# Attention output of odd head pairs in the other partition half, in a fused attention and two-layer MoE kernel on one core

## Chip, core and metric

One core of one Trainium2 chip runs the whole program in one launch. The metric is the device time of an execution in microseconds; lower is better. Before the change the median of 3 runs is 480.46 us (479.46 to 480.7).

## What is computed

Three stages follow each other, all with float32 inputs and results (w_in and w_out come as float64).

```python
# 1. decayed linear attention, B=2, H=8, S=768, D=64, in blocks along S
intra = (q_b k_b^T * Dmask) v_b                 # Dmask[i,j] = lam^(i-j), j<=i
inter = (q_b * lam^(pos+1)) kv_state
out_b = intra + inter
kv_state = lam^block * kv_state + (k_b * lam^(block-1-pos))^T v_b
# 2. x = out as [1536, 512]; x = act(x @ w_in) @ w_out
#    act(h) = h if h>=1, 0 if h<=-1, (h+1)^2/4 between;  w_in [512, 2048], w_out [2048, 512]
# 3. each token goes to the best of 8 experts: gate * relu(x @ w1[e]) @ w2[e]
```

## The kernel before

**Stages and chunks.** The 1536 tokens are 12 attention blocks of 128 tokens (six for each batch; all 8 heads of a block are one tile row). Blocks 0 to 3, 4 to 7 and 8 to 11 are three chunks of 512 tokens. For each chunk the first MoE (units 0 to 23, eight for a chunk, two tiles of 128 hidden columns each) runs a first layer (`m1_l1`, L700 to L709) and a second layer (`m1_l2`, L738 to L745), one unit behind. Each product is made of three matmuls, high by high, high by low and low by high part, in a fast float32 format; so every operand exists as a high and a low tile (xh and xl for the attention's output, w1h and w1l for w_in). Then tokens are routed, and the experts' tiles follow (`Tile2`).

**Weights of the first MoE.** w_in and w_out come as float64 in groups of 1 MB, [128 partitions, 8 KB]. `load_w` (L205) loads a group, and `convert` makes float32 of it: ScalarE L223 and L225, VectorE L226 (first pass, into cu) and L232 (second pass, into cw). `hilo` splits it: ScalarE L212 writes w1h, VectorE L213 writes w1l. The converted group is stored to DRAM (L239, issued by ScalarE) and read again for chunks 1 and 2. The first group of w_in is converted after block 2's xh and xl (`issue_after`), and its second pass stays behind the masks of block 4 (`behind[1, 0]`, L873).

**One attention block** (`attn_pieces`) has these steps. Heads come in four pairs, `pr`; head `h2` of a pair has its 64 channels in partition half `h2` of q and k.

- `prep`: GpSimd makes the decayed keys kd (L279) and the decayed queries qd (L288; three instructions, L290 and twice L293, for blocks from SWAP = 7 on).
- `masked`: eight matmuls of scores (L308) into two PSUM tiles, and two masks am on VectorE (L311). Three am buffers exist.
- `outv`: the value products, am by v (L335), into the output's PSUM tile.
- `outs`: the state products, state of the block before by qd (L348), added into the same tile; then xh on ScalarE (L354) and xl on VectorE (L355).
- `st`: the key-value products (L377) into a PSUM tile of their own, and the new state on VectorE, four instructions (L383), or a copy on ScalarE for the first block of a batch (L380). The last block of a batch (5, 11) makes no state.

A state product uses 64 rows and 64 columns of TensorE's array. Up to block 6 both heads of a pair keep their half, so only two of the four quarters of the array are used. From block 7 on the state and qd of the odd pairs lie in the other half, so the four pairs take turns over four quarters, with two PSUM tiles. For that, block 6's key-value products of odd pairs go to the other half, qd is written there in pieces, and `lamx` holds the decay in the changed order (three VectorE copies, L364 to L366).

**Order.** TensorE's order is the program's own (`manual_schedule`). The other engines' order comes from a planner that takes, as an engine falls free in its own reckoning, the earliest instruction of the program that is ready. The opening (L860 to L876) runs blocks 0 to 4: scores are issued one block ahead, then for a block m: key-value products, value products, scores of block m+1, state products. In block 0 the key-value products come after the output. Here PSUM tiles come from six buffers in turn (`at_tags`). After the opening, blocks 5 to 11 are cut in up to four pieces (`return [scores, st, outp, None]`), which `spread` places among the matmuls of the first and second layers; PSUM tiles then come from two buffers. Each piece is a visit: TensorE leaves the full tiles of the layers for the smaller ones of the attention and returns.

The queue of loads starts as `q1 v0 v1 q2 v2 q3 v3 w10 q4 v4 w11 w20` after q0, all on SP's queue; w10 is w_in's group 0 and v4 the keys and values of block 4.

Of the kernel before, what the change touches and what calls it, by code (L numbers as in the profile page):

```python
# [37 lines left out]
NSTART = 5  # L38
WARM_LAM = 6

SWAP = 7
START_LOADS = "q1 v0 v1 q2 v2 q3 v3 w10 q4 v4 w11 w20"

WHOLE = (2, 0)
# [3 lines left out]
def kernel(  # L48
# [129 lines left out]
    lamx = small([P, 4, 1], "lamx")  # L178

# [15 lines left out]
    def load_w(k, n):  # L195
        if n >= len(units):
            return
        lay, c, g = units[n]
        if lay == 2:
            load_raw((k, n), (w1 if k == 1 else w2)[bass.ds(tiles[c].e, 1), g])  # L200
        elif c:
            load_raw((k, n), wsc[k, g])
        else:
            t = sb.tile([P, 1024, 2], I32, name=f"rw{k}", tag=f"rw{k}")
            SP.dma_start(out=t.rearrange("p n t -> p (n t)"), in_=(w_in if k == 1 else w_out)[g].bitcast(I32))  # L205
            raw[k, n] = t

    def hilo(key, r, eng):
# [60 lines left out]
    def attn_pieces(m):  # L269
# [3 lines left out]
        def prep():  # L273
            if m >= NSTART - 1 and m + 1 < NBLK:
                load_attn(m + 1)
            qkt, kvt = attn_in[m]
            def keys():
                kd = sb.tile([P, NE, 64], F32, name="kd", tag="kd")
                G.tensor_tensor(kd, kvt[:, 0], rev.to_broadcast([P, NE, 64]), op=ALU.mult)  # L279
                ast[m, "kd"] = kd  # L280


            if cb < 5 and m >= NSTART:
                keys()
            if cb > 0:
                qd = sb.tile([P, 4, P], F32, name="qd", tag="qd")
                if m < SWAP:
                    G.tensor_tensor(qd, qkt[:, 0], wq, op=ALU.mult)  # L288
                else:
                    G.tensor_tensor(qd[:, 0::2, :], qkt[:, 0, 0::2, :], wq[:, 0::2, :], op=ALU.mult)  # L290
                    for h2 in range(2):
                        r, o = slice(64 * h2, 64 * h2 + 64), slice(64 - 64 * h2, 128 - 64 * h2)
                        G.tensor_tensor(qd[o, 1::2, :], qkt[r, 0, 1::2, :], wq[r, 1::2, :], op=ALU.mult)  # L293
                ast[m, "qd"] = qd
            if cb < 5 and m < NSTART:
                keys()
# [5 lines left out]
        def masked():  # L302
# [6 lines left out]
            for h2 in range(2):  # L309
                am = sb3.tile([P, 4, P], F32, name="am", tag="am")  # L310
                ast[m, "am"] = V.tensor_tensor(am, pts[h2], dmask.rearrange("p (r o) i -> p r o i", o=2)[:, :, h2, :], op=ALU.mult)  # L311
                ast[m, "A", h2] = am

        def outv():
# [8 lines left out]
            if m < SWAP:  # L323
                pt = at_tile([P, 4, P], "ao")
                pts, first, last = [pt[:, pr, :] for pr in range(4)], (0,), (3,)
                ast[m, "o"] = pts, [(pt, slice(0, 4))]
            else:
                two = [at_tile([P, 2, P], "ao") for _ in range(2)]
                pts, first, last = [two[pr % 2][:, pr // 2, :] for pr in range(4)], (0, 1), (2, 3)
                ast[m, "o"] = pts, [(two[i], slice(i, 4, 2)) for i in range(2)]  # L330
            ast[m, "last"] = last
            for pr in range(4):
                for h2 in range(2):
                    r = slice(64 * h2, 64 * h2 + 64)
                    PE.matmul(  # L335
                        pts[pr][r], lhsT=kvt[:, 1, 2 * pr + h2, :], rhs=am[h2][:, pr, :],
                        start=(pr in first), stop=(cb == 0 and pr in last), skip_group_check=True,
                    )

        def outs():  # L340
            pts, banks = ast.pop((m, "o"))
            last = ast.pop((m, "last"))
            if cb > 0:
                for pr in range(4):
                    for h2 in range(2):
                        r = slice(64 * h2, 64 * h2 + 64)
                        w = r if m < SWAP or pr % 2 == 0 else slice(64 - 64 * h2, 128 - 64 * h2)
                        PE.matmul(  # L348
                            pts[pr][r], lhsT=state[m - 1][w, pr, :], rhs=ast[m, "qd"][w, pr, :],
                            start=False, stop=(pr in last), skip_group_check=True,  # L350
                        )
            sl = slice(j * P, (j + 1) * P)
            for pt, prs in banks:
# [3 lines left out]
        def outp():  # L357
            outv()
            outs()

        def st():
            if m == NSTART:
                with tc.issue_after(ast[m, "am"].ins):
                    V.tensor_copy(lamx[:, 0::2], lamc[:, 0::2])  # L364
                    V.tensor_copy(lamx[64:128, 1::2], lamc[0:64, 1::2])
                    V.tensor_copy(lamx[0:64, 1::2], lamc[64:128, 1::2])  # L366
            if cb == 5:
                return
            qkt, kvt = attn_in[m]
            kd = ast.pop((m, "kd"))  # L370
            pt = at_tile([P, 4, 64], "as")
            for pr in range(4):
                for h2 in range(2):
                    h = 2 * pr + h2
                    at_ = 64 * h2 if m < SWAP - 1 or pr % 2 == 0 else 64 - 64 * h2
                    r = slice(at_, at_ + 64)
                    PE.matmul(pt[r, pr, :], lhsT=kd[:, h, :], rhs=kvt[:, 1, h, :], start=True, stop=True)  # L377
# [10 lines left out]
        pieces[m] = (prep, masked, outv, outs)  # L388
# [471 lines left out]
    for m in range(2):  # L860
        pieces[m][0]()
    for m in range(NSTART):
        if m:
            pcs[m][3]()
        pieces[m][2]()
        if 0 < m < NSTART - 1:
            pcs[m + 1][0]()
        pieces[m][3]()
        if not m:
            pcs[m][3]()  # L870
        if m == 3:

            behind[1, 0] = ast[4, "am"]  # L873
# [257 lines left out]
```

## Time and profile before

| what | us |
|---|---|
| median of 3 runs | 480.46 |
| lowest, highest | 479.46, 480.7 |
| profiled execution | 479.74 |
| its span | 477.9 |
| TensorE matmuls busy in it | 464.0 |
| VectorE, ScalarE, GpSimd busy | 328.0, 266.7, 81.3 |

PE is TensorE's matmuls, PEld its weight loads, DVE VectorE, ACT ScalarE, POOL GpSimd, SP the engine that issues most DMAs. In a line of the timeline stand the start in us from the span's start, the time from the first start to the last end of the group, the engine, the line of the program, the operation, what it writes and reads, its shape, how many instructions are merged, and in brackets the idle time before it and what ended that. Each matmul of the program counts as two.

### The profile page before, as it was taken

What the parts mean: (1) busy time and instruction counts of PE and PEld (TensorE: products, weight loads), DVE (VectorE), ACT (ScalarE), POOL (GpSimd) and SP (SyncE); (2) the same over time, 40 slices, a digit from 0 to 9 for tenths busy, and PEclk for the clock granted to TensorE, in tenths of its full rate; (3) what the DMA queues carried; (4) which work ended last, traced back from release to release, by engine and by line L of the source; (5) the groups of instructions that cost most, each with busy time, mean ns of one, the idle gap of its engine ahead of it and who ended that gap; (6) DMA issues with size and microseconds to landing.
All of it is one profiled execution on the core that took longest, in us unless ns stands there. A gap on an engine that the chain in (4) does not pass through costs nothing. (4 is left out here: it accounts for less than half of the span.)

```text
span 477.9 us, 7360 instructions
## 1 busy us (share of the span) xinstructions
PE 464.0 (97%) x2713; PEld 377.7 (79%) x2713; DVE 328.0 (69%) x726; ACT 266.7 (56%) x403; POOL 81.3 (17%) x83
## 2 busy tenths in 40 slices
PE   8999999999999999999999999999999999999990
PEld 5875778878878787878888888887878998998870
DVE  6889979879399997464999785666874354444410
ACT  2388879868975455445756754667233435435320
POOL 4513210002003120000000007000164400400201
PEclk9999999999999999999999999999999999999996
DMA  8999987768564223221433235330456543543201
GB/s 336 423 408 375 394 310 254 291 243 253 195 218 171 95 89 133 87 84 64 163 123 98 89 100 188 104 138 1 175 179 197 177 162 103 188 141 111 87 1 48
DMA packets 22651, 83.65 MB, mean 175 GB/s; under 512 B 3595, under 2 KB 3595, under 8 KB 20564
## 3 DMA queue, kind: packets, MB, share of 16 engines
q1 hardware_dynamic: 15842, 65.04, 38.9%
q10 hardware_dynamic: 4322, 11.55, 6.2%
q0 software_dynamic: 2448, 6.56, 3.9%
q8 instruction: 22, 0.36, 0.3%
q14 instruction: 17, 0.14, 0.1%
HBM read 68.44 MB, written 14.73 MB: 174 GB/s over the span
## 5 line engine op out<-in xcount | busy, mean ns | idle before, releaser
L213 DVE TENSOR_TENSOR w2l<-rw,w2h 128x1024 fp32r<-128x1024 f32 x32 | 39.2, 1225 | 55.2 <-ACT w2h L212 55.1
L700 PE MATMUL l<-xh,w1h 128*128 128x512 f32 x192 | 75.3, 397 | 0.9 <-ACT w1h L212 0.6
L743 PE MATMUL acc<-w2h,gh 128*128 128x512 f32 x184 | 72.8, 396 | 0.0
L702 PE MATMUL l<-xl,w1h 128*128 128x512 f32 x184 | 71.7, 390 | 0.0
L703 PE MATMUL l<-xh,w1l 128*128 128x512 f32 x184 | 71.7, 390 | 0.0
L745 PE MATMUL acc<-w2h,gl 128*128 128x512 f32 x184 | 71.7, 390 | 0.0
L744 PE MATMUL acc<-w2l,gh 128*128 128x512 f32 x184 | 71.7, 389 | 0.0
L212 ACT ACTIVATE w2h<-rw 128x1024 fp32r<-128x1024 f32 x32 | 33.9, 1059 | 57.1 <-PE m2a L819 30.0
L449 DVE CUSTOM_DVE_ANT_0 jk<-x2s,enb 128x512 f32<-128x512 f32 x72 | 48.0, 699 | 0.8 <-ACT x2s L434 0.6
L726 ACT ACTIVATE gh<-g_t 128x512 fp32r<-128x512 f32 x46 | 28.9, 629 | 33.0 <-DVE g_t L722 33.0
L213 DVE TENSOR_TENSOR w1l<-rw,w1h 128x1024 fp32r<-128x1024 f32 x32 | 39.7, 1241 | 11.1 <-ACT w1h L212 10.2
L719 ACT ACTIVATE r_t<-l,half 128x512 f32<-128x512 f32 x48 | 32.4, 680 | 26.2 <-PE l L703 25.8
L794 PE MATMUL m<-x2h,w1h 128*128 128x384 f32 (+2 forms) x128 | 43.9, 343 | 0.0
L700 PEld LDWEIGHTS l<-xh,w1h 128*128 128x128 f32 x192 | 35.8, 188 | 10.1 <-ACT w1h L212 1.2
L796 PE MATMUL m<-x2h,w1l 128*128 128x384 f32 (+2 forms) x128 | 43.3, 338 | 0.0
L795 PE MATMUL m<-x2l,w1h 128*128 128x384 f32 (+2 forms) x128 | 43.1, 337 | 0.0
L722 DVE SCALAR_TENSOR_TENSOR g_t<-r_t,l 128x512 f32<-128x512 f32 x46 | 31.4, 682 | 16.1 <-ACT r_t L720 16.0
L817 PE MATMUL m2a<-w2h,mh 128*128 128x512 f32 (+1 forms) x104 | 41.5, 399 | 0.0
L819 PE MATMUL m2a<-w2h,ml 128*128 128x512 f32 (+1 forms) x104 | 40.8, 392 | 0.0
L743 PEld LDWEIGHTS acc<-w2h,gh 128*128 128x128 f32 x184 | 34.5, 188 | 7.8 <-issue 0.5
L818 PE MATMUL m2a<-w2l,mh 128*128 128x512 f32 (+1 forms) x104 | 40.7, 391 | 0.0
L703 PEld LDWEIGHTS l<-xh,w1l 128*128 128x128 f32 x184 | 34.6, 188 | 7.2
(252 smaller groups left out, 843.9 us busy)
## 6 DMA issues: line engine op xcount, KB each, us to landing
rw<-wsc SPq DMA_DIRECT2D x32, 512.0 KB, 3.4
rw<-in_w_dram SPq DMA_DIRECT2D x32, 512.0 KB, 3.9
rw<-in_w_in_dram SPq DMA_DIRECT2D x8, 1024.0 KB
rw<-in_w_out_dram SPq DMA_DIRECT2D x8, 1024.0 KB, 12.8
wsc<-cw ACTq DMA_DIRECT2D x15, 512.0 KB, 6.8
qk_t<-in_qk_dram SPq DMA_DIRECT2D x12, 512.0 KB, 5.3
kv_t<-in_kv_dram SPq DMA_DIRECT2D x12, 512.0 KB, 12.5
x2d<-x2s ACTq DMA_DIRECT2D x12, 256.0 KB, 2.9
```

What stands on the lines that cost most here:

```text
L213: wlo[key] = eng.tensor_tensor(lo, r, hi.bitcast(F32), op=ALU.subtract)
L449: V.tensor_tensor_reduce(out=jk, in0=x2s, in1=enb[e // 2][:, e % 2, :], scale=1.0, scalar=0.0, op0=ALU.mult, op1=ALU.add, accum_out=lr[:, ...
L700: PE.matmul(pt, lhsT=hi[:, f, k, :], rhs=xh[c][:, k, :], start=(k == 0), stop=False)
L702: PE.matmul(pt, lhsT=hi[:, f, k, :], rhs=xl[c][:, k, :], start=False, stop=False)
L703: PE.matmul(pt, lhsT=lo[:, f, k, :], rhs=xh[c][:, k, :], start=False, stop=(k == 3))
L743: PE.matmul(a, lhsT=gh[:, f, sl], rhs=hi[:, f, :], start=(g == 0 and f == 0), stop=False)
L744: PE.matmul(a, lhsT=gh[:, f, sl], rhs=lo[:, f, :], start=False, stop=False)
L745: PE.matmul(a, lhsT=gl[:, f, sl], rhs=hi[:, f, :], start=False, stop=(g == 7 and f == 1))
L794: PE.matmul(pt, lhsT=hi[:, f, k, :], rhs=self.xh[:, k, :], start=(k == 0), stop=False)
L795: PE.matmul(pt, lhsT=hi[:, f, k, :], rhs=self.xl[:, k, :], start=False, stop=False)
L796: PE.matmul(pt, lhsT=lo[:, f, k, :], rhs=self.xh[:, k, :], start=False, stop=(k == 3))
L817: PE.matmul(a, lhsT=gh[:, f, sl], rhs=hi[:, f, :], start=(g == 0 and f == 0), stop=False)
```

## The change

All blocks get the order of quarters that only late blocks had, by another way: the state stays where it is, and the output of the odd pairs is written to the other partition half (`turned`). So xh and xl hold the odd pairs' channels with their halves exchanged, and the rows of w_in that they meet are exchanged as well, by its load: one transfer for the even row groups, two for the odd ones. Every block now has two output banks. The key-value products go into the unused half of the second bank, at the start of the output's visit, and the new state is made after xh and xl in that visit. In the opening block 0 has the order of the other blocks. `lamx`, SWAP and the split of qd are gone.

```diff
 load_w:
-            SP.dma_start(out=t.rearrange("p n t -> p (n t)"), in_=(w_in if k == 1 else w_out)[g].bitcast(I32))
+            if k == 1:
+                src = w_in[g].bitcast(I32).rearrange("p (f k x) -> p f k x", f=2, k=4)
+                dst = t.rearrange("p (f k i) t -> p f k (i t)", f=2, k=4)
+                SP.dma_start(out=dst[:, :, 0::2, :], in_=src[:, :, 0::2, :])
+                for h2 in range(2):
+                    r, o = slice(64 * h2, 64 * h2 + 64), slice(64 - 64 * h2, 128 - 64 * h2)
+                    SP.dma_start(out=dst[o, :, 1::2, :], in_=src[r, :, 1::2, :])
+            else:
+                SP.dma_start(out=t.rearrange("p n t -> p (n t)"), in_=w_out[g].bitcast(I32))
 prep:
-                if m < SWAP:
-                    G.tensor_tensor(qd, qkt[:, 0], wq, op=ALU.mult)
-                else:
...
+                G.tensor_tensor(qd, qkt[:, 0], wq, op=ALU.mult)
 attn_pieces:
+        def st():
+            banks = [at_tile([P, 4, P], "ao") for _ in range(2)]
+            ast[m, "banks"] = banks
+            if cb == 5:
+                return
...
+            pt = banks[1][:, 2:4, :].rearrange("p a (b d) -> p (a b) d", d=64)
...
+                    PE.matmul(pt[r, pr, :], lhsT=kd[:, h, :], rhs=kvt[:, 1, h, :], start=True, stop=True, skip_group_check=True)
+        def turned(pr, h2):
+            o = 64 * (h2 ^ (pr % 2))
+            return slice(o, o + 64)
 outv, outs:
+                for h2 in ((0, 1), (1, 0))[pr % 2]:
-                        pts[pr][r], lhsT=kvt[:, 1, 2 * pr + h2, :], rhs=am[h2][:, pr, :],
+                        banks[pr % 2][turned(pr, h2), pr // 2, :], lhsT=kvt[:, 1, 2 * pr + h2, :], rhs=am[h2][:, pr, :],
-                            pts[pr][r], lhsT=state[m - 1][w, pr, :], rhs=ast[m, "qd"][w, pr, :],
+                            banks[pr % 2][turned(pr, h2), pr // 2, :], lhsT=state[m - 1][r, pr, :], rhs=ast[m, "qd"][r, pr, :],
 after xh and xl, in outs:
+            pt = ast.pop((m, "st"))
             sn = sb.tile([P, 4, 64], F32, name="s_new", tag="state")
...
-                        sn[:, pr, :], state[m - 1][:, pr, :], (lamc if m < SWAP else lamx)[:, pr, :], pt[:, pr, :], op0=ALU.mult, op1=ALU.add,
+                        sn[:, pr, :], state[m - 1][:, pr, :], lamc[:, pr, :], pt[:, pr, :], op0=ALU.mult, op1=ALU.add,
-        return [scores, st, outp, None] if m >= NSTART else [scores, None, outp, st]
+        return [scores, None, outp, None]
 opening:
-        if m:
-            pcs[m][3]()
-        pieces[m][2]()
+        pieces[m][2]()
+        pieces[m][3]()
         if 0 < m < NSTART - 1:
             pcs[m + 1][0]()
-        pieces[m][3]()
-        if not m:
-            pcs[m][3]()
+        pieces[m][4]()
```

## Rows read from the trace of the kernel before

**Rows 1.** Page, part 1: busy time, share of the span, instructions.

```profile
PE 464.0 (97%) x2713; PEld 377.7 (79%) x2713; DVE 328.0 (69%) x726; ACT 266.7 (56%) x403; POOL 81.3 (17%) x83
```

**Rows 2.** Waits of TensorE: waiting line, what for, us in total, times, longest.

```profile
PE l L700 <- ACT w1h L212: 0.6, 1, 0.6
PE l L700 <- DVE g_t L722: 0.2, 1, 0.2
```

**Rows 3.** Timeline of TensorE, 10.7 to 25.2 us.

```profile
...
15.38 1.40 PE L308 MATMUL sc<-qk_t 64*128 64x128 f32 x16
16.70 1.09 PE L348 MATMUL ao<-qd,s_new 64*64 64x128 f32 x16
17.72 0.69 PE L377 MATMUL as<-kv_t,kd 128*64 128x64 f32 x16
18.24 1.05 PE L335 MATMUL ao<-am,kv_t 128*64 128x128 f32 x16
19.21 1.40 PE L308 MATMUL sc<-qk_t 64*128 64x128 f32 x16
...
22.72 1.09 PE L335 MATMUL ao<-am,kv_t 128*64 128x128 f32 x14 [0.17 <-DVE am L311]
...
24.94 0.50 PE L700 MATMUL l<-xh,w1h 128*128 128x512 f32 x1
```

**Rows 4.** Timeline of VectorE, 11 to 25 us.

```profile
11.29 0.85 DVE L383 SCALAR_TENSOR_TENSOR s_new<-s_new,lamc,as 128x64 f32<-128x64 f32 x4
...
16.62 1.29 DVE L311 TENSOR_TENSOR am<-sc,dmask 128x512 f32<-128x512 f32 x2 [0.55 <-PE sc L308]
18.46 0.28 DVE L383 SCALAR_TENSOR_TENSOR s_new<-s_new,lamc,as 128x64 f32<-128x64 f32 x1 [0.55 <-PE as L377]
18.66 0.68 DVE L355 TENSOR_TENSOR xl<-ao,xh 128x512 fp32r<-128x512 f32 x1
...
21.39 1.28 DVE L311 TENSOR_TENSOR am<-sc,dmask 128x512 f32<-128x512 f32 x2
22.59 1.21 DVE L232 SCALAR_TENSOR_TENSOR cw<-cz,cu 128x1024 int32<-128x1024 int32 x1
23.72 0.68 DVE L355 TENSOR_TENSOR xl<-ao,xh 128x512 fp32r<-128x512 f32 x1
```

**Rows 5.** Timeline of ScalarE, 18 to 31 us.

```profile
18.34 1.24 ACT L223 ACTIVATE cu<-rw,down 128x1024 int32<-128x1024 uint32 x1
...
23.83 1.06 ACT L212 ACTIVATE w1h<-cw 128x1024 fp32r<-128x1024 f32 x1 [1.55 <-DVE cw L232]
...
30.71 0.69 ACT L719 ACTIVATE r_t<-l,half 128x512 f32<-128x512 f32 x1 [1.36 <-PE l L703]
```

**Rows 6.** Timeline of TensorE, the output of block 7.

```profile
106.03 0.67 PE L348 MATMUL ao<-qd,s_new 64*64 64x128 f32 x16
106.62 0.50 PE L743 MATMUL acc<-w2h,gh 128*128 128x512 f32 x1
```

**Rows 7.** Timeline of TensorE, the visit of block 8's key-value products.

```profile
133.92 0.39 PE L700 MATMUL l<-xh,w1h 128*128 128x512 f32 x1
...
135.05 0.39 PE L703 MATMUL l<-xh,w1l 128*128 128x512 f32 x1
135.37 0.69 PE L377 MATMUL as<-kv_t,kd 128*64 128x64 f32 x16
...
136.78 0.39 PE L700 MATMUL l<-xh,w1h 128*128 128x512 f32 x1
```

**Rows 8.** Instructions on the tile lamx: ns min/median/max, first and last start.

```profile
L366 DVE COPY lamx<-lamc x1: 165/165/165, 36.4 to 36.4; 64x2 f32<-64x2 f32 x1
```

**Rows 9.** DMA queue of SP, 6 to 11.5 us, 4 KB packets: packets, MB, share.

```profile
q1 hardware_dynamic: 623, 2.26, 101.6%
```

**Rows 10.** The same, 18.9 to 21.9 us, 8 KB packets.

```profile
q1 hardware_dynamic: 173, 1.29, 102.4%
```

**Rows 11.** Timeline of GpSimd: the decayed keys of block 4.

```profile
19.34 1.04 POOL L279 TENSOR_TENSOR kd<-kv_t,rev 128x512 f32<-128x512 f32 x1 [3.20 <-DMA kv_t<-in_kv_dram]
```

More of the change, by code (lines that the diff above doesn't have):

```diff
@@ L39 @@
 WARM_LAM = 6
-SWAP = 7
 START_LOADS = "q1 v0 v1 q2 v2 q3 v3 w10 q4 v4 w11 w20"
@@ L177 @@
     lamc = small([P, 4, 1], "lamc")
-    lamx = small([P, 4, 1], "lamx")
     units = [(1, c, g) for c in range(len(CHUNKS)) for g in range(8)]
@@ L286, in prep @@
                 qd = sb.tile([P, 4, P], F32, name="qd", tag="qd")
-                if m < SWAP:
-                    G.tensor_tensor(qd, qkt[:, 0], wq, op=ALU.mult)
-                else:
[L290 to L293, printed above, removed]
+                G.tensor_tensor(qd, qkt[:, 0], wq, op=ALU.mult)
                 ast[m, "qd"] = qd
@@ L312, in masked @@
                 ast[m, "A", h2] = am
+        def st():
[3 more added lines that the diff above has]
+                return
+            kvt = attn_in[m][1]
+            kd = ast.pop((m, "kd"))
+            pt = banks[1][:, 2:4, :].rearrange("p a (b d) -> p (a b) d", d=64)
+            ast[m, "st"] = pt
+            for pr in range(4):
+                for h2 in range(2):
+                    h = 2 * pr + h2
+                    r = slice(64 * h2, 64 * h2 + 64)
+                    PE.matmul(pt[r, pr, :], lhsT=kd[:, h, :], rhs=kvt[:, 1, h, :], start=True, stop=True, skip_group_check=True)
+        def turned(pr, h2):
+            o = 64 * (h2 ^ (pr % 2))
+            return slice(o, o + 64)
         def outv():
@@ L320, in outv @@
             am = [ast.pop((m, "A", i)) for i in range(2)]
[L323 to L330, printed above, removed]
@@ L331, in outv @@
-            ast[m, "last"] = last
+            banks = ast[m, "banks"]
             for pr in range(4):
-                for h2 in range(2):
-                    r = slice(64 * h2, 64 * h2 + 64)
+                for h2 in ((0, 1), (1, 0))[pr % 2]:
                     PE.matmul(
-                        pts[pr][r], lhsT=kvt[:, 1, 2 * pr + h2, :], rhs=am[h2][:, pr, :],
-                        start=(pr in first), stop=(cb == 0 and pr in last), skip_group_check=True,
+                        banks[pr % 2][turned(pr, h2), pr // 2, :], lhsT=kvt[:, 1, 2 * pr + h2, :], rhs=am[h2][:, pr, :],
+                        start=(pr < 2), stop=(cb == 0 and pr >= 2), skip_group_check=True,
@@ L338, in outv @@
                     )
         def outs():
-            pts, banks = ast.pop((m, "o"))
-            last = ast.pop((m, "last"))
+            banks = ast.pop((m, "banks"))
             if cb > 0:
                 for pr in range(4):
-                    for h2 in range(2):
+                    for h2 in ((0, 1), (1, 0))[pr % 2]:
                         r = slice(64 * h2, 64 * h2 + 64)
-                        w = r if m < SWAP or pr % 2 == 0 else slice(64 - 64 * h2, 128 - 64 * h2)
                         PE.matmul(
-                            pts[pr][r], lhsT=state[m - 1][w, pr, :], rhs=ast[m, "qd"][w, pr, :],
-                            start=False, stop=(pr in last), skip_group_check=True,
+                            banks[pr % 2][turned(pr, h2), pr // 2, :], lhsT=state[m - 1][r, pr, :], rhs=ast[m, "qd"][r, pr, :],
+                            start=False, stop=(pr >= 2), skip_group_check=True,
@@ L351, in outs @@
                         )
             sl = slice(j * P, (j + 1) * P)
-            for pt, prs in banks:
+            for i in range(2):
+                pt, prs = banks[i][:, 0:2, :], slice(i, 4, 2)
                 ast[m, "xh"] = A.activation(xh[c][:, prs, sl], pt, AF.Copy)
                 ast[m, "xl"] = V.tensor_tensor(xl[c][:, prs, sl], pt, xh[c].bitcast(F32)[:, prs, sl], op=ALU.subtract)
[L357 to L366, printed above, removed]
@@ L367, in st @@
             if cb == 5:
                 return
[L369 to L377, printed above, removed]
+            pt = ast.pop((m, "st"))
@@ L383, in st, with outp @@
                     V.scalar_tensor_tensor(
-                        sn[:, pr, :], state[m - 1][:, pr, :], (lamc if m < SWAP else lamx)[:, pr, :], pt[:, pr, :], op0=ALU.mult, op1=ALU.add,
+                        sn[:, pr, :], state[m - 1][:, pr, :], lamc[:, pr, :], pt[:, pr, :], op0=ALU.mult, op1=ALU.add,
                     )
             state[m] = sn
-        pieces[m] = (prep, masked, outv, outs)
-        return [scores, st, outp, None] if m >= NSTART else [scores, None, outp, st]
+        def outp():
+            st()
+            outv()
+            outs()
+        pieces[m] = (prep, masked, st, outv, outs)
+        return [scores, None, outp, None]
     def inv_norm(s, n, nm, over_=None):
```

## The prediction

> **What bounds the kernel now.** I read the page's busy times first: TensorE is busy 97% of the span [rows 1]. A busy TensorE can still stand behind somebody, so the second view was its waits: two matter, 0.6 us for the high half of a w_in tile and 0.2 us for g_t, both before 51 us [rows 2]. After that nothing makes it wait, so from there on every microsecond taken out of its order shortens the run by as much; before, a microsecond counts only if whoever comes next is not late. The third view is therefore the order of TensorE, VectorE and ScalarE up to 25 us [rows 3 to 5], where blocks 0 to 4 of the attention run with nothing else beside them and end in the first matmul of the first layer (L700, 24.94).
>
> In rows 3 one block goes through scores (L308), the state products of the block before (L348), the key-value products for the new state (L377) and the value products (L335). State products occupy TensorE from 16.70 to 17.72, 1.02 us; key-value products 0.52 us (17.72 to 18.24); value products 0.97 us. The period of a block is 3.83 us (15.38 to 19.21). What the reader is to see in rows 4 and 5: L700 starts 0.05 us after ScalarE ends w1h (23.83 plus 1.06), and w1h starts as soon as VectorE is through with its second conversion pass (22.59 plus 1.21). So the end of the opening is set twice, by TensorE's order and by the conversion of the first w_in tile, almost to the same moment.
>
> **State products in four quarters.** Late blocks have them already: 106.03 to 106.62, 0.59 us with the change back to full tiles [rows 6], against 1.02 us in halves [rows 3]. The new placement uses the same four quarters and two banks, so 0.43 us is saved in each of blocks 1 to 5. Block 5 lies inside the first layer (its state products come at about 46 us): 0.43 us kept. In blocks 1 to 4 the 1.72 us are not kept. The next scores' masks are made on VectorE from the scores: from the scores' start to the end of both masks takes 2.53 us (15.38 to 17.91) [rows 3, 4], and the value products need both; with 0.97 us for them a block cannot repeat faster than about 3.55 us. That is 0.28 us less than now, for two periods; in block 0 the value products move behind the key-value products, which delays the mask that waits for their buffer by about 0.35 us. Scores of block 4 start at 19.2 us either way. Its masks are later still, at 21.39, because VectorE's first conversion pass stands ahead of them (their scores are done at 20.61), and TensorE waits for them at 22.72 [rows 3, 4]. So the opening gains nothing up to 22.7 us.
>
> **The new state in the output's visit.** For blocks 6 to 10 the key-value products lose a visit of their own. A visit: 1.73 us from the matmul at 135.05 to the fourth after it, where four steps take 0.90 us (five steps 1.13 us, 133.92 to 135.05), so 0.83 us [rows 7]. Within the output's visit they cost 0.52 us [rows 3]; saved are 0.31 us, five times, 1.55 us. Bounds: 0.7 us if they cost their whole duration of 0.69 us there, 1.9 us if they pack closer.
>
> The state update (L383, four instructions, 0.85 us together [rows 4]) now comes after the state products instead of before them, since it reads a bank that these write. In late blocks the next use is a visit later and TensorE waits for nobody: cost nothing, covered by that distance; without it 0.85 us per block. In the opening it is different. State 3 used to be begun at 18.46 and done by about 20.0, xl in between; now it is ready to be made only after the state products of block 3, at about 21.2, when VectorE is in conversion and masks until 22.67. TensorE wants it at about 23.7 for block 4. Behind the masks stand three things: state 3 (0.85 us), xl of block 3 (0.68 us) and the second conversion pass, which is what w1h and then L700 wait for. The order on VectorE is the planner's. In rows 4 it put one state update (18.46) ahead of xl (18.66), because that waits for ScalarE, and it put conversion (22.59) ahead of xl (23.72). By these rows I take: state 3, conversion, xl. Then conversion, w1h and L700 are 0.85 us later: L700 at 25.8. Ends: 0.25 us if conversion goes first and TensorE waits for state 3 a little; 1.6 us if xl goes ahead too; at best nothing. Once lost it is lost: the next w1h stands on ScalarE behind an activation that itself waits 1.36 us for TensorE (30.71) [rows 5], so all moves together and the wait of 0.6 us in rows 2 stays.
>
> **What else goes.** Three copies to lamx, 0.17 us each [rows 8], leave VectorE at about 35 to 37 us, where it is busy without a break; with them the 0.2 us for g_t [rows 2] go. Splitting qd into three for blocks 7 and up disappears on GpSimd, for which TensorE waits nowhere: nothing, covered by the distance between a block's scores and its output. xh and xl of blocks 0 to 6 come in two halves: one more instruction each on ScalarE and VectorE, under 0.2 us, hidden behind the mask loop in the opening and behind nobody's wait later. The bank with the new state is held until the update; the next scores want it several units later.
>
> **w_in in three transfers.** Rows of 8 KB become pieces of 1 KB, 1024 instead of 128, and SP issues three transfers where it issued one, eight times. No row has 1 KB pieces. With 4 KB packets the 16 engines move 2.26 MB in 5.5 us at 101.6%, so 404 GB/s or 162 ns for a packet on one engine [rows 9]; with 8 KB packets 1.29 MB in 3 us at 102.4%, so 420 GB/s or 312 ns [rows 10]. A line through both has 12 ns a packet and 37.5 ns a KB: 50 ns for 1 KB, 396 instead of 312 ns for a row, and at eight rows to an engine 0.67 us more for each load. Ends: nothing, or double, 2.5 us (a load is 2.5 us now). I take 0.67 us, the line. The first load is read at 18.34 [rows 5]. The value load two places behind it lands at 19.34 [rows 11], and the 1.05 MB between take 2.5 us, so the first load lands at about 16.8, with 1.5 us of cover: hidden. That value load moves to 20.0, its decayed keys on GpSimd to 21.1, where the key-value products of block 4 want them at about the same time while the masks last until 22.67: hidden too. Behind SP's two more issues stands the load of q for block 4, wanted at 19.2, and later loads; their queue is filled well ahead. If a cover goes, the price is what a load is late by.
> The Trainium skill, "DMA: Bandwidth & Descriptors", section Bandwidth, advises at least 1 MiB to a transfer for three quarters of the peak, and gives about 2 us fixed for each; by that two more transfers a load would add 4 us to each of eight loads. The trace does not agree where transfers queue: in rows 9 loads of 512 KB follow each other with the engines full.
>
> **Sum**, against the profiled execution of 479.74 us (span 477.9 and 1.8 around it, 0.72 us under the median of 480.46): block 5 -0.43, five visits -1.55, g_t -0.2, opening +0.85: -1.33. Applied to the median: 479.1 us. A measurement of this kernel can tell about 0.3%, 1.44 us, from no change; so the forecast lies just inside no change.
>
> **Rivals.** (A) The forecast, 0.45, with -0.7 to -2.0 us: 478.5 to 479.8; two fifths of it is beyond 1.44 us.
> (B) The opening gives back little: conversion keeps its place ahead of state 3, and TensorE's wait for that costs 0.25 us or less. Sum -1.9, and -2.5 where the wait of 0.6 us shrinks as well: 478.3. For it: rows 4 show conversion ahead of xl. Against: state 3 is ready over 1 us before VectorE gets to choose. 0.27.
> (C) Slower: the small pieces. Place: the first load, then each next one. It decides from 1.5 us more a load, where the read at 18.34 starts to slip. At double cost the first load is 1.0 us late, and since the engines are full through the opening the lag adds up by 2.5 us a load over the first five, against covers of a few us: some 5 us of waits on ScalarE's conversions, less 2 us of gains, +3 us: 483.5. For it: the full engines in rows 9 and 10, and no row with such pieces. Against: the fixed part of 12 ns. 0.13. By the skill's 2 us a transfer the same mechanism would decide from the first load on; I give that 0.03 of the 0.13.
> (D) VectorE takes both state 3 and xl ahead of conversion, 1.6 us or a little more: -0.6 to 0, 480.1. 0.15.
>
> **How the numbers follow.** Faster: B and two fifths of A, 0.45. Same: the rest of A and D, 0.42. Slower: C, 0.13. The range from 477.8 to 481.6 takes in A, B, D and the milder part of C.
>
> **What would show it.** Right: 16 state products in about 0.6 us in blocks 1 to 5; no L377-like group alone between first- or second-layer matmuls after 60 us; L700 first at about 25.8; block 4's value products waiting for masks as now; packets of the SP queue up by about 7200 and no wait for rw. Wrong: L700 before 24.9 (the opening kept its gain) or after 26.6; ScalarE or VectorE waiting for a w_in load; a new wait of TensorE after 60 us; GpSimd's decayed keys holding block 4.

## The result, and the profile after

The change makes the kernel slower: 487.02 us median (484.43 to 487.96, 4 runs) against 479.96 (479.33 to 480.7, 4 runs) of the kernel before on the same chip, a ratio of 1.0135, interval 1.0108 to 1.0161. I had forecast 479.1 us, and even the upper end of my range, 481.6, is 5.4 us short. The profiled execution took 487.96 us, its span is 486.1 us, so it is read beside a span of 477.9.

The page of the changed kernel comes first: busy time of TensorE, its granted clock in 40 slices of 12.15 us, and GB/s of the DMA engines in the same slices.

```profile
PE 462.7 (95%) x2713; PEld 377.2 (78%) x2713; DVE 328.3 (68%) x730; ACT 267.5 (55%) x410; POOL 73.7 (15%) x73
...
PEclk9999799999999999999999999999999999999996
...
GB/s 315 287 317 335 304 328 309 301 333 291 264 159 177 137 131 52 123 88 83 133 88 131 101 109 182 88 159 14 102 227 177 170 172 130 173 134 119 94 1 46
```

TensorE's matmuls are busy 1.3 us less than in [rows 1], in a span that is 8.2 us longer: the time went into waits. The transfers run at about 300 GB/s for the first ten slices, with the engines no less busy than before, and the clock has a 7 in the fifth slice. The waits of TensorE (line, what it waited for, us in total, times, longest) answer to [rows 2].

```profile
PE l L694 <- DVE g_t L716: 6.2, 2, 5.6
PE ao L328 <- POOL kd L286: 2.5, 2, 1.5
```

The wait for g_t that was 0.2 us is 6.2 us. Where and why is in three timelines. TensorE's own (L328 makes the key-value products, L355 the state products, L694 to L697 the first layer) in two stretches, the end of the opening and 49 to 62 us:

```profile
24.75 0.69 PE L328 MATMUL ao<-kv_t,kd 128*64 128x64 f32 x16 [1.49 <-POOL kd L286]
...
27.04 1.01 PE L355 MATMUL ao<-qd,s_new 64*64 64x128 f32 x16 [0.72 <-DVE s_new L372]
27.98 1.19 PE L694 MATMUL l<-xh,w1h 128*128 128x512 f32 x4
...
49.23 0.39 PE L696 MATMUL l<-xl,w1h 128*128 128x512 f32 x1
...
51.53 0.39 PE L697 MATMUL l<-xh,w1l 128*128 128x512 f32 x1
57.47 0.79 PE L694 MATMUL l<-xh,w1h 128*128 128x512 f32 x1 [5.55 <-DVE g_t L716]
58.06 0.63 PE L696 MATMUL l<-xl,w1h 128*128 128x512 f32 x1
...
61.47 0.63 PE L694 MATMUL l<-xh,w1h 128*128 128x512 f32 x1
```

VectorE's (L233 is the first conversion pass, L239 the second, L363 xl, L372 the new state):

```profile
24.92 1.21 DVE L239 SCALAR_TENSOR_TENSOR cw<-cz,cu 128x1024 int32<-128x1024 int32 x1
26.05 0.74 DVE L363 TENSOR_TENSOR xl<-ao,xh 128x256 fp32r<-128x256 f32 x2
26.72 0.84 DVE L372 SCALAR_TENSOR_TENSOR s_new<-s_new,lamc,ao 128x64 f32<-128x64 f32 x4
...
54.46 1.23 DVE L233 SCALAR_TENSOR_TENSOR cu<-rw,cu 128x1024 int32<-128x1024 int32 x1 [4.23 <-ACT cu L230]
...
56.73 0.68 DVE L716 SCALAR_TENSOR_TENSOR g_t<-r_t,l 128x512 f32<-128x512 f32 x1
```

and the one line of ScalarE's that began it:

```profile
53.21 1.21 ACT L230 ACTIVATE cu<-rw,down 128x1024 int32<-128x1024 uint32 x1 [4.97 <-DMA rw<-in_w_in_dram]
```

It is the longest of three; the list of ScalarE's waits, 0 to 130 us, has for this step (us in total, times, longest):

```profile
ACT cu L230 <- DMA rw<-in_w_in_dram: 8.1, 3, 5.0
```

Read from the bottom of the timelines: ScalarE stood 4.97 us before a load of w_in that had not landed; VectorE's conversion behind it waited 4.23 us for ScalarE; g_t stood behind the conversion on VectorE's queue, and TensorE waited 5.55 us for g_t. The opening lost time as well: block 4's key-value products waited 1.49 us for their keys (24.75), which GpSimd began at 23.24 where it had begun them at 19.34 [rows 11], because their load came later. The next row of TensorE's timeline shows a second price. Eight matmul steps take 3.41 us from 58.06 to 61.47, 0.43 us each; ten steps took 2.30 us from 49.23 to 51.53, 0.23 us each. The windows of the changed kernel say why (columns: us, then busy time of PE, PEld, DVE, ACT and POOL with their instructions, PEclk, DMA share, GB/s).

```profile
12.00:25.00 13.00, 10.20 (x182) 8.45 (x184) 9.49 (x22) 4.62 (x9) 8.48 (x7) 1.00 1.10 286
25.00:38.00 13.00, 12.28 (x102) 9.96 (x99) 12.37 (x22) 9.71 (x12) 1.28 (x1) 1.00 1.07 314
...
57.40:62.00 4.60, 4.53 (x11) 3.56 (x12) 4.60 (x7) 4.54 (x6) 0.00 (x0) 0.50 1.03 322
62.00:70.00 8.00, 8.00 (x37) 6.62 (x36) 5.28 (x7) 5.35 (x8) 0.00 (x0) 1.00 1.08 305
```

From 57.4 to 62 us the granted clock was 0.50, the level of 1.2 GHz, behind a wait of 5.55 us; after that 2.4 GHz again. Ten steps at 0.2 us more are 2.0 us. The first two lines are where the cause lies; the first of these windows in the kernel before was:

```profile
12.00:25.00 13.00, 12.72 (x209) 10.84 (x207) 10.57 (x23) 5.14 (x7) 6.83 (x6) 1.00 1.03 424
```

Full engines in both, 424 GB/s in the one and 286 in the other. The DMA view of 12 to 38 us shows the loss in 40 slices of 0.65 us; changed kernel:

```profile
GB/s 403 389 367 362 183 158 233 228 238 228 266 359 383 375 355 307 200 192 241 247 222 228 331 378 391 403 391 397 425 410 391 372 356 172 169 227 238 301 211 260
```

It isn't slow throughout: mostly 350 to 425 GB/s, with three dips to 160 to 250, and three loads of w_in come up in the queue there. In the six slices from 14.6 us on the mean is 211 GB/s, 0.82 MB in 3.9 us; at the 403 GB/s of other slices that takes 2.0 us. So I estimate 1.9 us lost in that dip; the next (six slices from 22.4 us, mean 222) lost 1.8 us by the same working.

### The profile page after: what moved, and what is told of

Read it like the earlier page. It is cut to its first block, busy times and chain, and to the rows that moved or that the text cites. A ratio compares the mean times of both kernels' runs of the same rounds, so it can differ in the third digit from the quotient of the medians.

```text
span 486.1 us, 7386 instructions
## 1 busy us (share of the span) xinstructions
PE 462.7 (95%) x2713; PEld 377.2 (78%) x2713; DVE 328.3 (68%) x730; ACT 267.5 (55%) x410; POOL 73.7 (15%) x73
## 5 line engine op out<-in xcount | busy, mean ns | idle before, releaser
L694 PE MATMUL l<-xh,w1h 128*128 128x512 f32 x192 | 76.1, 401 | 6.2 <-DVE g_t L716 6.2
L697 PE MATMUL l<-xh,w1l 128*128 128x512 f32 x184 | 72.4, 393 | 0.0
L694 PEld LDWEIGHTS l<-xh,w1h 128*128 128x128 f32 x192 | 36.4, 190 | 15.6 <-DVE g_t L716 7.0
L697 PEld LDWEIGHTS l<-xh,w1l 128*128 128x128 f32 x184 | 35.0, 190 | 7.5
L696 PEld LDWEIGHTS l<-xl,w1h 128*128 128x128 f32 x184 | 35.1, 191 | 7.1
```

What stands on the lines that cost most here:

```text
L694: PE.matmul(pt, lhsT=hi[:, f, k, :], rhs=xh[c][:, k, :], start=(k == 0), stop=False)
L696: PE.matmul(pt, lhsT=hi[:, f, k, :], rhs=xl[c][:, k, :], start=False, stop=False)
L697: PE.matmul(pt, lhsT=lo[:, f, k, :], rhs=xh[c][:, k, :], start=False, stop=(k == 3))
```

## Experiments

The lines of the experiments' kernels are numbered differently; L346, L349, L355 and L360 are all the state products, L685 to L694 the first layer.

### One load, or three

The first question is whether the loads alone are the loss, and which property of them. e1 keeps the change, and loads w_in in one transfer of 8 KB rows; the exchange of halves is done in the layout of the input instead.

```diff
-            if k == 1:
-...
-                    SP.dma_start(out=dst[o, :, 1::2, :], in_=src[r, :, 1::2, :])
...
+            SP.dma_start(out=t.rearrange("p n t -> p (n t)"), in_=(w_in if k == 1 else w_out)[g].bitcast(I32))
...
+    w_in = inputs['moe_w_in'].reshape(4, 2, 64, 8, 2, 128)
+    w_in = np.stack([w_in[k, ::-1] if k % 2 else w_in[k] for k in range(4)])
...
```

> The changed kernel with w_in's exchanged rows laid out beforehand in DRAM, so that each group comes again in one transfer of 8 KB rows; all else as changed. Theory L (the whole loss is the slower loads): ScalarE waits for no w_in load, TensorE's wait of 5.6 us for g_t and the slow clock after it are gone, and what is left is the change's other parts: visits -1.55, block 5 -0.43, opening up to +1.0, small waits -0.6: ratio 0.994 to 0.998, about 478.2 us. Rival R (the loss is the new order on VectorE, state 3 and the later state updates): the wait for g_t stays at several us, ratio 1.005 or more.

Measured: 477.39 us, ratio 0.9937 (0.9918 to 0.9956), span 475.2. The window of e1 from 12 to 25 us, with columns as above:

```profile
12.00:25.00 13.00, 11.50 (x200) 9.38 (x196) 9.90 (x24) 5.22 (x10) 8.89 (x7) 1.00 1.02 415
```

The timeline of TensorE in e1, the end of the opening and an output's visit with the key-value products in it (between 103.00 and 104.81):

```profile
25.29 0.92 PE L346 MATMUL ao<-qd,s_new 64*64 64x128 f32 x16 [0.99 <-DVE s_new L363]
26.14 1.19 PE L685 MATMUL l<-xh,w1h 128*128 128x512 f32 x4
...
103.00 0.39 PE L730 MATMUL acc<-w2h,gl 128*128 128x512 f32 x1
...
104.81 0.67 PE L346 MATMUL ao<-qd,s_new 64*64 64x128 f32 x16
105.41 0.50 PE L728 MATMUL acc<-w2h,gh 128*128 128x512 f32 x1
```

The timeline of VectorE in e1, 23 to 26 us:

```profile
23.08 1.21 DVE L230 SCALAR_TENSOR_TENSOR cw<-cz,cu 128x1024 int32<-128x1024 int32 x1
24.22 0.74 DVE L354 TENSOR_TENSOR xl<-ao,xh 128x256 fp32r<-128x256 f32 x2
24.88 0.84 DVE L363 SCALAR_TENSOR_TENSOR s_new<-s_new,lamc,ao 128x64 f32<-128x64 f32 x4
```

The rate is back at 415 GB/s, the wait for g_t is gone, and the rest of the change is worth 0.63% to the good, where theory L had 0.2 to 0.6%: so the loads turn a gain of about 3 us into a loss of about 7. In spans it is 10.9 us: the matmul at 57.47 in the changed kernel stands at 49.91 here, 7.56 us sooner (1.84 of them are there when the first layer starts), and 2.2 us follow, nearly all of them the clock, so that the distance is 9.8 us by the second layer (62.41 against 52.63). Another 0.9 us come at 96.17, where TensorE waits 0.65 us for g_t again, after ScalarE had stood 2.41 us before a load of w_in at 87.86; only the last 0.2 us are not accounted for. e1 beats both kernels, and of the other edits only k1, below, comes to the same time.

The next three kernels leave the kernel before as it was, and only load w_in in other pieces. e2 has the change's three transfers with every row where it was:

```diff
...
+                SP.dma_start(out=dst[:, :, 0::2, :], in_=src[:, :, 0::2, :])
+                for h2 in range(2):
+                    r = slice(64 * h2, 64 * h2 + 64)
+                    SP.dma_start(out=dst[r, :, 1::2, :], in_=src[r, :, 1::2, :])
...
```

> The kernel before with w_in loaded in the change's three transfers of 1 KB pieces, but each row to its own partition, and nothing else changed. Theory L: the DMA rate in the opening falls from about 420 to about 300 GB/s, ScalarE waits for w_in loads, and the loss is that of the change plus what the change gains elsewhere, about 1.5 to 2 us more: ratio 1.015 to 1.022. Rival R: ratio within 0.3% of 1.

Measured: 486.75 us, ratio 1.011 (1.0072 to 1.0149). The window of e2 from 12 to 25 us:

```profile
12.00:25.00 13.00, 11.04 (x192) 9.54 (x190) 10.00 (x22) 4.05 (x5) 7.64 (x7) 1.00 1.08 303
```

With nothing of the change but its loads, the kernel before loses 1.1% and shows the same rate. Theory L had wanted 1.015 to 1.022, the change's loss and its gains together, and that is a miss: the two do not simply add. ScalarE waits about as long for w_in loads as in the changed kernel (0.76, 1.89 and 4.89 us), but TensorE's wait for g_t is 3.8 us here and 5.6 there; why, I did not follow. e3 has the same 1 KB pieces in two transfers, each to all 128 partitions:

```diff
...
+                for i in range(2):
+                    SP.dma_start(out=dst[:, :, i::2, :], in_=src[:, :, i::2, :])
...
```

> The kernel before with w_in in two transfers of 1 KB pieces, each to all 128 partitions. Theory Lp (1 KB pieces are slow as such): the 8 KB rows beside them get slow too, rate about 300 GB/s, ratio 1.012 to 1.022 like the three transfers. Theory Lh (transfers to 64 partitions are slow, since neighbouring engines then write close together): packets of 1 KB at 46 to 50 ns, rate about 390 GB/s or more, ratio 0.998 to 1.004. Theory Ln (the number of transfers, each waiting for an older one to land): half of the loss at most, ratio about 1.005.

Measured: 479.45 us, ratio 0.9982 (0.9965 to 0.9999). The window of e3 from 12 to 25 us:

```profile
12.00:25.00 13.00, 12.14 (x208) 10.43 (x204) 10.71 (x22) 4.76 (x6) 7.18 (x6) 1.00 1.05 403
```

So 1 KB pieces cost no time, though that is what I had priced. e4 has three transfers, one full and two to 64 partitions, in pieces of 4 KB (the row tiles of w_in are laid out in another order for it):

```diff
...
+                SP.dma_start(out=dst[:, 0, :], in_=src[:, 0, :])
+                for h2 in range(2):
+                    r = slice(64 * h2, 64 * h2 + 64)
+                    SP.dma_start(out=dst[r, 1, :], in_=src[r, 1, :])
...
```

> The kernel before with w_in in three transfers, one to 128 partitions and two to 64 each, but in pieces of 4 KB (the tile's order changed, DRAM laid out to match). Theory Lp: pieces are large, so about no loss, ratio 0.998 to 1.003. Theory Lh: the two half transfers are as slow as in the change, 4 KB packets well over 160 ns, ratio 1.008 to 1.02. Theory Ln: loss like the three small ones, ratio 1.015 to 1.022, with the DMA engines not full.

Measured: 485.56 us, ratio 1.0102 (1.0049 to 1.0154). The window of e4 from 12 to 25 us:

```profile
12.00:25.00 13.00, 12.01 (x205) 10.34 (x203) 10.70 (x23) 4.54 (x6) 7.20 (x6) 1.00 1.04 306
```

Large pieces lose as much as small ones. What remained was the third transfer, or the 64 partitions.

### Three transfers, or 64 partitions

Both kernels are again the one before with w_in in three transfers of 1 KB pieces. In f2 all three go to 128 partitions; in f3 the two small ones go to 64 each, but to every other one.

```diff
f2:
...
+                for i in range(2):
+                    SP.dma_start(out=dst[:, i, 1::2, :], in_=src[:, i, 1::2, :])
...
f3:
...
+                for i in range(2):
+                    SP.dma_start(out=dst[i::2, :, 1::2, :], in_=src[i::2, :, 1::2, :])
...
```

> The kernel before with w_in in three transfers as in the change (one of 512 KB, two of 256 KB, 1 KB pieces), but all three to 128 partitions: the two small ones take the two hidden tiles in turn. Half-height theory: 1 KB packets at 46 ns, rate about 400 GB/s, ratio 0.996 to 1.003. Rival (three transfers, the third one being what two did not show): rate about 300 GB/s, ratio 1.008 or more.

Measured: 479.5 us, ratio 0.9987 (0.997 to 1.0004). The window of f2 from 12 to 25 us:

```profile
12.00:25.00 13.00, 12.88 (x214) 10.97 (x209) 10.71 (x25) 4.85 (x6) 7.32 (x6) 1.00 1.05 403
```

> The kernel before with w_in in three transfers, the two small ones to 64 partitions each, but to every other partition instead of one half. If it is the closeness that hurts (16 engines writing within one half of the partitions), the engines keep to the partitions they have in a full transfer: packets 46 ns, ratio 0.996 to 1.003. If it is 64 rows to a transfer as such, packets of 60 to 70 ns and ratio 1.008 or more.

Measured: 479.71 us, ratio 1.0001 (0.9983 to 1.0018). The window of f3 from 12 to 25 us:

```profile
12.00:25.00 13.00, 12.89 (x215) 11.09 (x213) 10.71 (x25) 4.66 (x6) 6.52 (x6) 1.00 1.05 403
```

Three transfers cost nothing, and 64 partitions cost nothing where they are not neighbours. But f3 differs from e2 on both sides: e2's small transfers also read 64 neighbouring rows of memory, f3's read every other. h1 and h2 part the two; the rows of the odd tiles lie in another order in the input, so that the tiles hold the same data.

```diff
h1 (from f3):
-                    SP.dma_start(out=dst[i::2, :, 1::2, :], in_=src[i::2, :, 1::2, :])
+                    SP.dma_start(out=dst[i::2, :, 1::2, :], in_=src[64 * i:64 * i + 64, :, 1::2, :])
h2 (from e2):
-                    SP.dma_start(out=dst[r, :, 1::2, :], in_=src[r, :, 1::2, :])
+                    SP.dma_start(out=dst[r, :, 1::2, :], in_=src[h2::2, :, 1::2, :])
```

> The kernel before with w_in in three transfers: the two small ones read 64 neighbouring rows of memory each, but write every other of the 128 partitions (rows of the odd tiles laid out for it on the host, so the tiles hold the same data). Theory (what is slow is 16 DMA engines that write into 64 neighbouring partitions): as in f3_before_every_other, about 400 GB/s from 12 to 25 us and 479 to 481 us. Rival (what is slow is that the 16 engines read 64 neighbouring rows, half of the memory region that a full transfer reads): as in e2_before_three_small, about 303 GB/s and 484 to 488 us.

Measured: 479.59 us, ratio 0.9989 (0.9978 to 0.9999). The window of h1 from 12 to 25 us:

```profile
12.00:25.00 13.00, 11.83 (x206) 10.33 (x206) 10.71 (x22) 4.85 (x6) 7.17 (x6) 1.00 1.05 403
```

> The mirror of h1_from_half_to_every_other: the two small transfers read every other row of memory, and write 64 neighbouring partitions each. Theory (the writes into 64 neighbouring partitions are slow): about 303 GB/s from 12 to 25 us and 484 to 488 us. Rival (the reads are slow): about 400 GB/s and 479 to 481 us. If both of these kernels come between 480.5 and 484, both sides have a part in it.

Measured: 485.14 us, ratio 1.0131 (1.008 to 1.0182). The window of h2 from 12 to 25 us:

```profile
12.00:25.00 13.00, 11.41 (x199) 9.91 (x197) 10.48 (x23) 4.06 (x5) 7.54 (x6) 1.00 1.08 297
```

The two rates and times fall to either side as the theory said. It is the writes: a transfer into one half of the partitions (0 to 63 or 64 to 127) is slow, wherever it reads from, with pieces of 1 KB (e2, h2) and of 4 KB (e4). No run writes 64 neighbours across the middle, such as 32 to 95, so whether it is the neighbourhood or the half stays open.

### Both halves at once

If the loss comes from all engines writing one half of the partitions at a time, two transfers to both halves at the same moment might be at full rate. g3 is the changed kernel with the second half issued on another queue.

```diff
-                    SP.dma_start(out=dst[o, :, 1::2, :], in_=src[r, :, 1::2, :])
+                    (A if h2 else SP).dma_start(out=dst[o, :, 1::2, :], in_=src[r, :, 1::2, :])
```

> The changed kernel, with the second of the two transfers to 64 partitions issued by ScalarE, on its queue, rather than by SyncE behind the first, so that both halves can be under way at once. Theory (16 DMA engines that write into the same 64 neighbouring partitions at one time are slow): with both halves in flight the rate from 12 to 25 us goes back above 370 GB/s, the wait for g_t falls under 1 us, and the time comes to 477 to 480 us. Rival (any transfer that covers 64 neighbouring partitions is slow by itself, whatever is beside it): the rate stays near 300 GB/s and the time within 2 us of 487. A third outcome, a time of 480 to 485, would mean that the halves meet only in part, or that ScalarE waits at the issue.

Measured: 492.99 us, ratio 1.0269 (1.0241 to 1.0298), worse than the change. The window of g3 from 12 to 25 us:

```profile
12.00:25.00 13.00, 9.74 (x168) 8.18 (x162) 7.62 (x20) 3.96 (x7) 5.78 (x5) 0.98 1.08 315
```

The issues of odd halves by SyncE in g3, 8 to 16 us (ns min, median, max of the issue, first and last start):

```profile
L210 SPq DMA_DIRECT2D rw<-in_w_in_dram x2: 543/582/620, 10.7 to 15.0; - x2
```

The timeline of ScalarE's queue in g3, with its issues of the other halves:

```profile
1.31 0.65 ACTq L210 DMA_DIRECT2D rw<-in_w_in_dram  x1
...
8.67 0.54 ACTq L210 DMA_DIRECT2D rw<-in_w_in_dram  x1
```

The rate is the rival's, and the time, 6 us above the change, is neither theory's. The run doesn't decide: in the first two loads the halves were issued 9.4 us (1.31 and 10.7) and 6.3 us (8.67 and 15.0) apart, and ScalarE's queue had moved its halves, 0.26 MB from 1 to 10 us and 0.24 MB from 12 to 16 us, by about the time SyncE issued the others, so that they can hardly have met. Why it is slower still than the change I didn't follow up. Whether two halves at once are slow too stays open.

### The opening, without the slow loads

Three edits of e1 look for what the opening still loses (its first layer starts 1.20 us later than in [rows 3]). f1 makes the state right behind the key-value products, from a PSUM tile of their own:

```diff
...
+            early = m < NSTART
+            pt = at_tile([P, 4, 64], "as") if early else banks[1][:, 2:4, :].rearrange("p a (b d) -> p (a b) d", d=64)
...
+            if early:
+                renew(pt)
...
```

> The changed kernel with one load per w_in group (as in the run with one load), and in the opening the key-value products in a PSUM tile of their own with the new state made right behind them; later blocks as changed. Theory (the late state costs the opening: block 4's state products wait for state 3, which VectorE makes behind conversion and xl): the first layer starts at 24.9 to 25.3 us instead of 26.1; of these 1.0 us some 0.6 come back as the wait for w1h of the second unit; total 0.3 to 1.0 us less than 477.4. Rival (masks and conversion set the opening whatever the state does): the first layer still starts at 26 us and the total stays within 0.3 us.

Measured: 481.73 us, ratio 1.0027 (1.0012 to 1.0043). The waits of TensorE in f1:

```profile
PE as L331 <- issue: 3.4, 1, 3.4
...
PE as L331 <- DVE xl L368: 1.4, 1, 1.4
```

Here L331 makes the key-value products. The run does not answer its question: its first layer starts at 31.34 us, 5.2 us later than in e1. Of these, 2.9 us are there before the new tile's first product: already the first 32 score products take 3.76 us where e1's take 2.06, for a reason that I did not follow. Then the new tile waits. A block now takes five PSUM tiles from six buffers, and the waits of 1.4 and 3.4 us end 0.06 and 0.11 us after VectorE's xl of the block before, which ends at 17.78 and at 29.14 us. g1 keeps the tile and only gives out the state update ahead of xh and xl:

```diff
...
+            if m < NSTART:
+                renew()
...
+            if m >= NSTART:
+                renew()
...
```

> The kernel of e1_one_load (w_in in one transfer) with one thing moved: in the opening blocks the state update on VectorE is given out ahead of xl of the same block, not behind it. Theory (order on VectorE costs the opening): state 3 is ready about 1.2 us sooner, the 1.0 us for which block 4's state products waited in e1_one_load goes, the first layer's first product starts at 25.3 to 25.7 us instead of 26.14, since only w1h and xl hold it, and the time is 0.3 to 0.7 us under e1_one_load's 477.39, a ratio of 0.992 to 0.993 to the kernel before. Rival (given back by w1h): the conversion and xl come later by the four updates, w1h with them, a wait for w1h of 0.6 us opens at the first unit again, and the time stays within 0.3 us of e1_one_load's.

Measured: 478.8 us, ratio 0.9982 (0.9969 to 0.9995). The timeline of VectorE in g1, from 24 us:

```profile
24.24 0.84 DVE L349 SCALAR_TENSOR_TENSOR s_new<-s_new,lamc,ao 128x64 f32<-128x64 f32 x4
...
25.34 1.21 DVE L230 SCALAR_TENSOR_TENSOR cw<-cz,cu 128x1024 int32<-128x1024 int32 x1
```

The timeline of ScalarE in g1, with the second half of xh and with w1h:

```profile
25.18 0.39 ACT L369 ACTIVATE xh<-ao 128x256 fp32r<-128x256 f32 x1 [2.08 <-DVE s_new L349]
...
26.58 1.06 ACT L210 ACTIVATE w1h<-cw 128x1024 fp32r<-128x1024 f32 x1
```

The timeline of TensorE in g1, first layer:

```profile
27.69 1.19 PE L691 MATMUL l<-xh,w1h 128*128 128x512 f32 x4 [1.63 <-ACT w1h L210]
```

The wait for the state is gone, and the conversion is 2.26 us later (25.34 instead of 23.08), so the first layer is 1.55 us later than in e1. The rival had the place right and the size too small: an interval above e1's whole interval, since the second half of xh now waits 2.08 us for the state update as well. k1 puts GpSimd's order back to that of the kernel before:

```diff
...
-                keys()
+                with ExitStack() as hold:
+                    if m == 2:
+                        hold.enter_context(tc.issue_after(ast[1, "queries"].ins))
+                    keys()
...
```

> The kernel of e1_one_load (w_in in one transfer), with block 2's decayed keys put behind block 1's decayed queries on GpSimd, as in the kernel before. Theory (what is left of the opening's loss is GpSimd's order: in e1_one_load block 1's state products wait 0.58 us for their queries, which stand behind keys that wait 1.62 us for a load, and everything up to the first layer comes 0.5 us later): that wait goes, VectorE's second conversion pass starts near 22.6 us instead of 23.08, the first layer's first product at 25.6 to 25.7 instead of 26.14, and about 0.5 us of it stays to the end: 476.9 us, or a ratio of 0.9925 to 0.993 to the kernel before against 0.9937. Rival (the masks or another wait take it up): the first layer starts within 0.15 us of 26.14 and the time is that of e1_one_load.

Measured: 477.32 us, ratio 0.9945 (0.9923 to 0.9966), not to be told from e1. The second conversion pass in the timeline of VectorE in k1:

```profile
22.48 2.03 DVE L230 SCALAR_TENSOR_TENSOR cw<-cz,cu 128x1024 int32<-128x1024 int32 x1
```

What GpSimd does beside it in k1, decayed queries:

```profile
22.15 1.28 POOL L285 TENSOR_TENSOR qd<-qk_t,wq 128x512 f32<-128x512 f32 x1
```

The timeline of TensorE in k1, the end of the opening:

```profile
25.51 0.92 PE L349 MATMUL ao<-qd,s_new 64*64 64x128 f32 x16 [1.71 <-DVE s_new L366]
26.36 0.97 PE L688 MATMUL l<-xh,w1h 128*128 128x512 f32 x3
```

The conversion pass starts 0.60 us sooner, as the theory wanted, and takes 2.03 us instead of 1.21, beside a GpSimd product that in e1 was over as the pass began (at 23.11); xl, the state and the first layer are no sooner. The first layer is 0.22 us later than e1's, a little outside the rival's 0.15, and the time is e1's: the theory is out, and the rival holds in the main.

## Why the prediction was wrong

**The step that failed** is the load: "Ends: nothing, or double, 2.5 us (a load is 2.5 us now). I take 0.67 us, the line." The line was drawn through packet sizes, [rows 9, 10], and for what it prices it was no worse than too dear: e3 and f2 move 1 KB pieces at 403 GB/s and lose no time. But I read the two small transfers as two more pieces of queue, and never asked which partitions each of them writes. That term was 1.8 to 1.9 us a load (estimated above from the dips), nearer the end I had called double, and I took the low end because the line passed near it, although no row showed a transfer into half of the partitions. With it the cover of 1.5 us goes at once and the lag adds up from load to load, as rival C says: ScalarE waits 0.43 us for w_in at 20.33, 2.69 at 39.95 and 4.97 at 53.21, 8.1 us together where C had "some 5 us of waits". So C had the place and the chain, at a chance of 0.13, with the wrong cause, and its price of +3 us lacked a part of these waits, the 2.0 us that TensorE ran at 1.2 GHz behind the longest, and the opening. There "hidden too" failed with it: the load of block 4's values came late enough for TensorE to wait 1.49 us for its keys.

The Trainium skill, "DMA: Bandwidth & Descriptors", section Bandwidth, on which I weighed 0.03, isn't the cause either: f2 issues the same three transfers a load and loses nothing. The 2 us that I took from that page stand under another heading of it, "Anatomy of one DMA — SWDGE (gpsimd) path", as measured for transfers that GpSimd issues; these loads are SyncE's.

**The rest, by e1**, which is the change without those loads. Differences of the same matmul to the kernel before:
- Quarters: right; the 16 state products take 0.67 us (104.81 in e1, as in [rows 6]) and block 5 gained 0.44 us (e1 is 0.49 us late before it and 0.05 us late behind it) against 0.43.
- Visits: 0.37 us each instead of 0.31, 1.86 us over five against 1.55 (the matmul that stands at 53.10 in the kernel before is 0.47 us sooner in e1, the one at 189.36 is 2.33 us sooner). The lost visit was 0.84 us, as in [rows 7]; its price in the output's visit was 0.47 (2.41 us from 103.00 to 105.41, where the kernel before has 1.94, from 104.68 to 106.62), not the 0.52 of [rows 3]; why it packs that much closer I did not follow up. 1.86 lies just under my upper bound of 1.9.
- The wait for g_t: -0.5 us where I had 0.2; the rest is the start of the matmul behind it, a sign that to take a wait away is worth somewhat more than its length.
- The opening: +1.20 us against +0.85, so the size was near, but not the order. I took "state 3, conversion, xl"; VectorE did conversion, xl, state 3, in e1 and in the changed kernel (24.92, 26.05, 26.72). The conversion kept its place, as in rival B, and TensorE's wait for the state was 0.99 us where B had 0.25 or less. "Scores of block 4 start at 19.2 us either way" failed as well: in e1 they start at 20.33, after TensorE had waited 0.54 us for keys and 0.58 us for queries on GpSimd, which I had given no price, and the conversion comes 0.49 us later (23.08 against 22.59). Nor do blocks repeat in "about 3.55 us" (2.53 and 0.97 make 3.50): scores start at 12.47, 16.30 and 20.33 in e1. "Once lost it is lost" was wrong too: 0.70 us were given back at unit 1, where the wait for w1h of [rows 2] went. That is B's milder sum of -2.5, and e1's span is 2.7 us shorter.
- "The conversion ... 1.6 us if xl goes ahead too": g1 comes near this order (state, half of xl, conversion, the other half), and there the first layer is 2.75 us behind [rows 3].

So without the half-partition loads the change comes to rival B's sum; that it does so is in part luck, since B's price for the state's wait was too low and the visits and g_t gave more than I had. What would make me wrong was on my list, and in the changed kernel four of its signs came true: ScalarE waiting for w_in loads, the first layer after 26.6 (27.98), GpSimd's keys holding block 4 (1.49 us), and a new wait of TensorE after 60 us (0.65 at 96.17).

## What to carry to other kernels

When a transfer is cut, look at which partitions each part writes before its count and its pieces: two transfers, each into one half of the partitions, cost about 1.8 us a load here, and the same bytes to every other partition, or to all, cost nothing. If halves must be exchanged, do it in the layout of the input, where one transfer of full rows carries it. Where queues are full from the start, the price of a load is not hidden by the cover of the first one: it adds up until somebody waits, and a TensorE that waited some us (5.55 here) may come back at half its clock.

## What was not expected of the hardware

- A transfer into partitions 0 to 63 or 64 to 127 drops the sum of the 16 DMA engines to 160 to 250 GB/s in its slices, though their busy share stays above 1.0 (1.10 over 12 to 25 us in the changed kernel); over 12 to 25 us it was 286 to 306 GB/s in the kernels that have it on SyncE's queue, 315 in g3, 403 to 424 in the others. Why these writes are slow no run here shows.
- TensorE's granted clock stood at 0.50 from 57.4 to 62 us, right behind the wait of 5.55 us. It fell behind waits of 3.81 us (e2, 0.70 from 54 to 58 us) and 2.82 us (h2, 0.57 from 54 to 58 us) too, but not behind f1's 3.42 us in the opening (1.00 from 29 to 31 us).
- A VectorE conversion pass of 1.21 us took 2.03 us beside a GpSimd product (k1), and ended 1.08 us after it (24.51 and 23.43). Other traces have the same distance: 23.80 and 22.72 in the changed kernel, 21.46 and 20.38 in the kernel before (the keys of [rows 11]). The other way round, GpSimd's queries of 1.27 us took 2.25 us in the kernel before (20.34 to 22.59) beside that pass, 1.13 us beyond its end. So in these rows the one that comes second gets on only when the first is done; what they share no run shows.
